# Delta rule and gated MLP on one core: state and read in one 128-column matmul, corners of two heads at a time

## The chip, the cores and the metric

The kernel runs on one core of a Trainium2 chip. The metric is the device time of one execution in microseconds; three executions of the kernel before took 574.62, 570.97 and 570.29 us, median 570.97. One more execution was taken under the hardware profiler. In its rows PE is the matrix engine (TensorE), PEld its loads of stationary operands, DVE the vector engine, ACT the scalar engine, POOL GpSimd, and SP the engine that only issues transfers.

## The reference

Two layers follow one another. The first is a delta rule per batch and head (4 batches, 8 heads, 768 tokens, head size 48), in order of the tokens, with `k` normalised:

```python
for t in range(S):
    y[:, :, t] = einsum('bhd,bhde->bhe', q[:, :, t], state)
    v_old = einsum('bhde,bhd->bhe', state, k[:, :, t])
    state = state + beta[t] * einsum('bhd,bhe->bhde', k[:, :, t], v[:, :, t] - v_old)
```

The outputs of the heads side by side are `x` (4 x 768 x 384). The second layer is a gated MLP that mixes tokens:

```python
h = gelu_tanh(x @ w_in)                 # 384 -> 1024
u, v = h[..., :512], h[..., 512:]
v_n = (v - mean(v)) / sqrt(var(v) + 1e-6) * g_ln
v_s = einsum('ts,bsd->btd', w_sg, v_n) + b_sg[None, :, None]
out = x + (u * v_s) @ w_out
```

## The kernel before

**Chunks.** The tokens are cut into chunks of 64 (`T`). There are two phases, each over two of the four batches with six chunks, so twelve chunks (`NCH`) in a row; a chunk is worked on in two halves `e = 0, 1`, and each half has two sides `sd` of eight heads. The two sides lie in partitions 0 to 63 and 64 to 127 (`TOK`; head rows in `OWN`). Every float32 matmul of the chain, the grams and the corners stands in the trace as two records, each with its weight load (384 matmuls of `own` are 768 rows).

**The triangular solve.** Inside a chunk the delta rule is a linear system with a unit triangular 64 x 64 matrix per head, made of the gram matrix of `k`. `gram` (L276) makes the grams of `k` with `k` and of `k` with `q` for the chunk seven turns ahead, in four quarters; each ends with one ACT copy of 512 elements into `GM` (L293). `gstore` sends the two 32 x 32 diagonal blocks to memory; `lanes` (L307) inverts them on DVE, one matrix per partition, as background work; `zfetch` brings the inverses into `Z`. The off-diagonal 32 x 32 block comes from two products per head, `corner_a` (L446) and `corner_b` (L461): 32 matmuls of 32 x 32 each, copied out by ACT (L459, L476). `above` (L250) masks the read matrix (the gram of `k` with `q`) on DVE.

**The chain of a chunk** (`chain`, L492), per half `e`:

- `old`: keys times the state, added on DVE to the scaled values `v` (L508);
- `ask`: queries times the state, into the bank of the read, dealt between the steps of `own`: `Z` times `v`, copied by ACT to `u` (L530);
- `state` (L536): keys times `u` (64 x 48 stationary) accumulate the state in the bank `cb`, copied by ACT to `S` (L543);
- `read` (L547): the masked matrix times `u` (64 x 64 stationary) accumulates on top of `ask`, copied by ACT to `xt` (L558). State and read are dealt step by step between one another.

**The MLP of a chunk** (`Ffn`, L648): `turn` transposes `xt` on TensorE and splits it into `xh` and `xl` (two buffers each); `values` (18 matmuls of 512 columns, named four or two at a time, L676) and `gate` (four, L640 to L642) are the projection with `w_in`, each product made of three matmuls of split operands.

**Order.** Nothing is left to a planner: every engine runs its instructions in the order in which the program names them. A loop over `TURNS` (L884) writes the order out: in each turn the steps of one chunk's chain are alternated with the MLP steps of an earlier chunk, so that TensorE has other work while ACT and DVE answer. The pair `(c, f)` names the chunk of the chain and the chunk of the MLP; turns 4 and 5 have no chain, and the transposes for the next turn's MLP are made in the turn before (L988). Background work on DVE (`lanes`, decoding of `w_in`) is let in by `tick`, by the estimates in `COST` and by `SHARE`. Loads are issued on POOL (`kload`, `qload`, `vload`, `tload`), the small transfers on SP. After the last turn follow the mixing over tokens (`spatial`) and the projection with `w_out` (`project`).

Of the kernel before, what the change touches and what calls it, by code (L numbers as in the profile page):

```python
# [21 lines left out]
T = 64  # L22
# [28 lines left out]
         *((c, c - 1) for c in range(4, NCH)), (None, NCH - 1))  # L51


@with_exitstack
def delta_rule_gmlp_kernel(
# [63 lines left out]
    GM = [(main if i < 4 else low).tile([P, NP, 2, T], F32, name=f"gm{i}") for i in range(N_M)]  # L119
# [4 lines left out]
    S = [main.tile([P, NH, HD], F32, name=f"s{i}") for i in range(N_2)]  # L124
    KT = [main.tile([P, NP, HD], F32, name=f"kt{i}") for i in range(N_2)]
# [21 lines left out]
    def tload(c):  # L147
        if c < NCH:
            load(nc.gpsimd, KT[c % N_2], ktok[c])
# [38 lines left out]
    gdt, zsrc, ztile, zds, zks, ns, nvs, ztks, j1s = {}, {}, {}, {}, {}, {}, {}, {}, {}  # L188
# [21 lines left out]

    def kgram(c):
        def phase(e):
# [9 lines left out]
            def done():  # L222
                nc.scalar.copy(out=GM[c % N_M][:, 8 * e:8 * e + 8, 0], in_=st["ps"])

# [4 lines left out]
    def gstore(c, queues):  # L229
# [5 lines left out]
        for half in range(2):  # L235
            for sd in range(2):
# [3 lines left out]
                    in_=GM[c % N_M][r0:r0 + 32, :, 0, 32 * half:32 * half + 32],  # L240
# [9 lines left out]
    def above(c):  # L250

        if c >= NCH:
            return
        m = GM[c % N_M][:, :, 1]
        nc.vector.tensor_tensor(out=m, in0=m, in1=later.unsqueeze(1).broadcast_to([P, NP, T]), op=ALU.mult)

    def qgram(c):
        def phase(e):
# [10 lines left out]
            def done():  # L269
                nc.scalar.copy(out=GM[c % N_M][:, js, 1], in_=st["ps"])  # L270

# [4 lines left out]
    def gram(c):  # L276
# [4 lines left out]
        def phase(qd):  # L281
# [10 lines left out]
            def done():  # L292
                nc.scalar.copy(out=GM[c % N_M][:, js], in_=st["ps"])  # L293
# [152 lines left out]
    def corner_a(c):  # L446
        if c >= NCH:
            return
        z, g = Z[c % N_Z], GM[c % N_M]
        j1s[c] = j1 = main.tile([P, 8, 32], F32, name="j1", bufs=2)  # L450
        ps = bank()[:, 0:256].rearrange("p (j t) -> p j t", t=32)
        for i in range(8):
            for odd in range(2):
                for sd in range(2):
                    a = slice(64 * sd + 32 * odd, 64 * sd + 32 * odd + 32)
                    b = slice(64 * sd + 32, 64 * sd + 64)
                    j = 2 * i + odd
                    mm(ps[a, i], g[b, j, 0, 0:32], z[b, j, 32:64])
        nc.scalar.copy(out=j1, in_=ps)  # L459

    def corner_b(c):  # L461
        if c >= NCH:
            return
        zx = Z[c % N_Z].rearrange("p (i x) t -> p x i t", x=2)
        j1, ztk = j1s.pop(c), ztks.pop(c)
# [677 lines left out]
```

## Time and profile before

| what | value |
|---|---|
| median of three executions | 570.97 us (570.29 to 574.62) |
| the profiled execution's own time | 572.43 us |
| its span, first to last instruction | 570.7 us |
| mean granted TensorE clock | 0.877 |
| PE busy | 452.5 us, 7763 records |
| PEld busy | 393.5 us, 7763 loads |
| DVE busy | 362.1 us, 1039 instructions |
| ACT busy | 172.5 us, 383 instructions |
| POOL busy | 83.2 us, 100 instructions |

Busy time counts an engine as busy while at least one of its instructions runs; records of TensorE overlap one another, so their lengths do not add up to its busy time. The chain of waits follows the work that ended last back to the start: at each step to what released it, or to the instruction before it on its engine. A row of the groups gives line, engine, operation, what is written from what, partitions x elements, the count, the busy time and the mean length, and the idle time before them with what ended it. For a matmul the two numbers after the tiles are rows x columns of the stationary operand.

### The profile page before, as it was taken

To read this page: it belongs to the slowest core of one execution; us is meant where nothing else is said; L and a number is where in the kernel's file an instruction comes from. 1 tells how busy PE (TensorE), PEld (TensorE's weight loads), DVE (VectorE), ACT (ScalarE), POOL (GpSimd) and SP (SyncE) were. 2 spreads that over 40 slices of the span, in tenths; PEclk is the share of its full clock that TensorE was granted. 3 is DMA by queue.
4 is the path that set the end of the run, shared out by engine and by line. 5 is a ranking of instruction groups with operands and counts; after the bars stand their busy time and mean duration, and the time that the engine had idled before them with its cause. 6 is when DMAs were issued, how large, how long until landed. Compare 5 with 4: busy or idle time off the path is not lost.

```text
span 570.7 us, 18015 instructions
## 1 busy us (share of the span) xinstructions
PE 452.5 (79%) x7763; PEld 393.5 (69%) x7763; DVE 362.1 (63%) x1039; ACT 172.5 (30%) x383; POOL 83.2 (15%) x100
## 2 busy tenths in 40 slices
PE   3134579656539762989989989799998999999997
PEld 2134356334437561878778778688997999999997
DVE  3994927316399995666987976873559657433422
ACT  2032224222234211342443444354343413111110
POOL 2311202002012000111021011000004223222220
PEclk8576669769578966788989999899999999999999
DMA  7697955449546406575684678743885762544113
GB/s 180 177 284 182 261 90 154 119 108 275 118 117 183 133 1 195 140 227 119 188 266 113 192 251 226 218 139 109 262 245 130 211 183 62 165 139 137 50 35 125
DMA packets 106239, 92.81 MB, mean 163 GB/s; under 512 B 71600, under 2 KB 83888, under 8 KB 106160
## 3 DMA queue, kind: packets, MB, share of 16 engines
q1 hardware_dynamic: 93264, 58.40, 36.8%
q0 software_dynamic: 8544, 31.72, 19.7%
q10 hardware_dynamic: 4352, 1.54, 1.1%
q8 instruction: 61, 1.00, 0.8%
q14 instruction: 18, 0.15, 0.1%
HBM read 63.30 MB, written 28.34 MB: 161 GB/s over the span
## 4 chain that ended last, share of the span: by engine, by line
PE 55%; DVE 17%; DMA 15%; issue 6%; SPq 4%; ACT 3%; ACTq 0%; POOL 0%; DVEq 0%; POOLq 0%
PE ps L81 17%; PE ps L640 10%; PE ps L642 9%; PE ps L641 9%; PE ps L676 5%; DMA z<-zd 5%; PE ps L98 3%; DVE ztmp L366 3%; DVE zl L373 3%; DMA vraw<-vD 2%; SPq L238 2%; DMA kd<-kqT 2%; DMA zd<-zl 2%; DMA zk<-zd 1%; DMA gd<-gm 1%
## 5 line engine op out<-in xcount | busy, mean ns | idle before, releaser
L81 PEld LDWEIGHTS ps<-s,kq 48*64 48x64 f32 x1408 | 49.7, 146 | 17.9 <-issue 10.8
L783 POOL TENSOR_TENSOR ga<-ga,uT 128x384 f32<-128x384 f32 x32 | 36.4, 1142 | 166.4 <-DVE ga L780 120.6
L81 PE MATMUL ps<-kd 48*64 48x128 f32 (+1 forms) x768 | 38.5, 327 | 27.5 <-DMA kd<-kqT 26.9
L81 PE MATMUL ps<-s,kq 48*64 48x48 f32 x1408 | 56.5, 232 | 0.0
L81 PEld LDWEIGHTS ps<-kd 48*64 48x64 f32 x768 | 33.2, 173 | 30.5 <-DMA kd<-kqT 20.1
L641 PE MATMUL ps<-xl,winh 128*128 128x256 f32 x144 | 43.6, 303 | 10.7 <-DVE xl L666 10.5
L366 DVE TENSOR_TENSOR ztmp<-zl 128x120 f32<-128x120 f32 (+26 forms) x180 | 48.7, 302 | 2.1
L373 DVE TENSOR_TENSOR zl<-zl,ztmp 128x120 f32<-128x120 f32 (+26 forms) x180 | 48.1, 300 | 0.8
L640 PE MATMUL ps<-xh,winh 128*128 128x256 f32 x144 | 46.8, 325 | 0.0
L508 DVE TENSOR_TENSOR v<-v,ps 128x384 f32<-128x384 f32 x22 | 12.1, 548 | 49.5 <-PE ps L81 49.5
L642 PE MATMUL ps<-xh,winl 128*128 128x256 f32 x144 | 43.1, 299 | 0.1
L645 ACT CAST gh<-ga 128x384 fp32r<-128x384 f32 x32 | 16.4, 511 | 78.9 <-POOL ga L783 63.6
L641 PEld LDWEIGHTS ps<-xl,winh 128*128 128x128 f32 x144 | 29.9, 208 | 12.3 <-DVE xl L666 12.1
L81 PE MATMUL ps<-v,z 64*64 64x48 f32 x768 | 30.4, 231 | 8.1 <-issue 4.2
L81 PE MATMUL ps<-z,gm 32*32 32x32 f32 x768 | 11.3, 208 | 32.1 <-DMA z<-zd 32.1
L646 DVE TENSOR_TENSOR gl<-ga,gh 128x384 fp32r<-128x384 f32 x32 | 18.1, 565 | 26.8 <-ACT gh L645 26.8
L81 PEld LDWEIGHTS ps<-z,gm 32*32 32x32 f32 x768 | 9.5, 119 | 35.7 <-issue 26.5
L81 PE MATMUL ps<-u,kt 64*48 64x48 f32 x704 | 23.0, 216 | 14.1 <-ACT u L530 8.9
L642 PE MATMUL ps<-wouth,gl 128*128 128x384 f32 x96 | 33.0, 347 | 1.3 <-DVE gl L646 1.3
L640 PE MATMUL ps<-wouth,gh 128*128 128x384 f32 x96 | 33.0, 346 | 1.2 <-ACT gh L645 1.2
L293 ACT COPY gm<-ps 128x512 f32<-128x512 f32 x40 | 21.8, 590 | 38.8 <-PE ps L81 31.5
L697 ACT ACTIVATE ut<-ps 128x256 f32<-128x256 f32 x48 | 18.4, 383 | 49.5 <-PE ps L642 42.1
(127 smaller groups left out, 1206.8 us busy)
## 6 DMA issues: line engine op xcount, KB each, us to landing
kq<-kqT POOLq DMA_DIRECT2D x12, 896.0 KB, 8.7
kd<-kqT POOLq DMA_DIRECT2D x10, 896.0 KB, 7.6
uD<-ut SPq DMA_DIRECT2D x12, 512.0 KB, 6.5
vD<-vg SPq DMA_DIRECT2D x24, 256.0 KB, 4.0
vraw<-vD SPq DMA_DIRECT2D x48, 128.0 KB, 3.1
uT<-uD SPq DMA_DIRECT2D x8, 768.0 KB, 5.0
v<-vtok POOLq DMA_DIRECT2D x12, 384.0 KB, 4.1
kt<-ktok POOLq DMA_DIRECT2D x12, 384.0 KB, 7.8
```

The source lines that it names most:

```text
L81: return nc.tensor.matmul(out=out, lhsT=lhsT, rhs=rhs, start=start, stop=stop, skip_group_check=True)
L98: nc.tensor.matmul(out=ps, lhsT=lhsT, rhs=busy, start=True, stop=True)
L293: nc.scalar.copy(out=GM[c % N_M][:, js], in_=st["ps"])
L366: tv.tensor_tensor(out=st["tmp"][:, at:at + m * (r1 - r0) * w].rearrange("p (m r t) -> p m r t", m=m, t=w), in0=z[:, :, r0:r1, i:i + 1].br ...
L373: tv.tensor_tensor(out=z[:, :, r0:r1, i + 1:32], in0=z[:, :, r0:r1, i + 1:32], in1=st["tmp"][:, at:at + m * (r1 - r0) * w].rearrange("p (m ...
L640: nc.tensor.matmul(out=ps, lhsT=sh, rhs=mh, start=(first and i == 0), stop=False)
L641: nc.tensor.matmul(out=ps, lhsT=sh, rhs=ml, start=False, stop=False)
L642: nc.tensor.matmul(out=ps, lhsT=sl, rhs=mh, start=False, stop=(last and i == n - 1))
L646: nc.vector.tensor_tensor(out=lo, in0=src, in1=hi.bitcast(F32), op=ALU.subtract)
L676: nc.tensor.matmul(out=self.ps, lhsT=(self.xl if k == 2 else self.xh)[:, cc, bi], rhs=(winl if k == 1 else winh)[:, cc, DH:], start=(i == ...
L697: nc.scalar.activation(out=self.ut[:, :, d].rearrange("p y e t -> p e y t"), in_=ps.rearrange("p e (y t) -> p e y t", t=T), func=AF.Gelu_a ...
L783: nc.gpsimd.tensor_tensor(out=gv, in0=gv, in1=uT[:, :, d], op=ALU.mult)
```

## The change

- `state` and `read` become one step. A tile `MK` (three of them, one per half-chunk) holds keys and masked read matrix of the eight heads in turn, 64 columns each, so that the keys of a head and its read matrix are 128 neighbouring columns, in one order for side 0 and in the other for side 1. One matmul per head and side writes state rows and read rows together. Each side has a bank of its own (`cb[sd]`), into which `ask` writes too. Both banks are copied out by ACT into `xt`, which now holds state and outputs; `S`, `KT` and the bank of the read are gone, and `xt` has two buffers for three.
- `tload` writes the keys of a half-chunk straight into `MK`, in two transfers; `above` writes the masked matrix there, half by half. The step of half 1 is moved behind `vprep`.
- The corners take two heads per matmul: `corner_a` has 64 stationary and 64 moving columns on 32 rows, of which the diagonal blocks are copied out (four copies) into a tile whose other blocks were set to zero; `corner_b` has 32 stationary and 64 moving columns on 64 rows, copied out by one copy on ACT and one on DVE.
- `GM` becomes three tiles: `GK` (columns 0 to 31 of the gram of `k`), `GE` (columns 32 to 63, two buffers) and `GQ` (the gram with `q`), by three ACT copies.
- The transposes work on 64 partitions and 64 columns each, 12 for 6. A table `TURNED` says in which turn a chunk is transposed: chunks 0 and 1 in turns 0 and 1 (before: 2 and 3), 2 and 3 in turns 3 and 4 (before: 4 and 5), the others as before.
- `xstore` is issued as two transfers; `COST` is lowered for the merged steps.

```diff
+TURNED = {0: 0, 1: 1, 3: 2, 4: 3, **{c + 2: c for c in range(4, NCH)}}
...
+    MK = [main.tile([P, 2 * NH + 1, T], F32, name=f"mk{i}") for i in range(3)]
+    J1 = [main.tile([P, 8, 2, 32], F32, name=f"j1{i}") for i in range(N_2)]
+    for t in (*MK, *J1):
+        nc.vector.memset(t, 0.0)
...
+    def tload(c, e):
+        if c >= NCH:
+            return
+        for r in range(2):
+            sd = r ^ e
+            nc.gpsimd.dma_start(
+                out=MK[(2 * c + e) % 3][TOK[r], 2 * sd:2 * sd + 2 * NH - 1:2, 0:HD],
+                in_=ktok[c, e, TOK[r]].rearrange("p (h d) -> p h d", d=HD))
...
+    def keep(c, js, ps):
+        for t, tile in enumerate((GK[c % N_M], GE[c % N_2])):
+            nc.scalar.copy(out=tile[:, js], in_=ps[:, :, 32 * t:32 * t + 32])
...
+        nc.vector.tensor_tensor(
+            out=MK[(2 * c + e) % 3][:, 1:2 * NH:2], in0=GQ[c % N_M][:, 8 * e:8 * e + 8],
+            in1=later.unsqueeze(1).broadcast_to([P, NH, T]), op=ALU.mult)
...
-                nc.scalar.copy(out=GM[c % N_M][:, js], in_=st["ps"])
+                keep(c, js, st["ps"][:, :, 0])
+                nc.scalar.copy(out=GQ[c % N_M][:, js], in_=st["ps"][:, :, 1])
...
         for i in range(8):
-            for odd in range(2):
-                for sd in range(2):
-                    a = slice(64 * sd + 32 * odd, 64 * sd + 32 * odd + 32)
-                    b = slice(64 * sd + 32, 64 * sd + 64)
-                    j = 2 * i + odd
-                    mm(ps[a, i], g[b, j, 0, 0:32], z[b, j, 32:64])
-        nc.scalar.copy(out=j1, in_=ps)
+            for sd in range(2):
+                b = slice(64 * sd + 32, 64 * sd + 64)
+                mm(ps[TOK[sd], i], g[b, 2 * i:2 * i + 2].rearrange("p x t -> p (x t)"), z[b, 2 * i:2 * i + 2, 32:64])
+        for odd in range(2):
+            for sd in range(2):
+                a = slice(64 * sd + 32 * odd, 64 * sd + 32 * odd + 32)
+                nc.scalar.copy(out=j1[a, :, odd], in_=ps[a, :, odd])
...
+            for sd in range(2):
+                mm(ps[64 * sd:64 * sd + 32, 2 * i:2 * i + 2], ztk[TOK[sd], i],
+                   j1[TOK[sd], i].rearrange("p x t -> p (x t)"))
+        for sd, copy in enumerate((nc.scalar.copy, nc.vector.tensor_copy)):
+            a = slice(64 * sd, 64 * sd + 32)
+            copy(out=z[a, :, 32:64], in_=ps[a])
...
                 for sd in range(2):
-                    r, j = sd ^ e, 8 * e + h
-                    mm(cb[OWN[sd], h], kt[TOK[r], j], u[TOK[r], j], start=(fresh[e] and h == 0))
+                    r = sd ^ e
+                    mm(cb[sd][:, h], mk[e][TOK[r], T * (2 * h + sd):T * (2 * h + sd + 2)], u[TOK[r], 8 * e + h],
+                       start=(fresh[e] and h == 0))
 
             def done():
-                mark(nc.scalar.copy(out=S[(2 * c + e + 1) % N_2][0:112], in_=cb[0:112]))
                 for sd in range(2):
+                    mark(nc.scalar.copy(
+                        out=xt[c][:, e, sd].rearrange("p (h e) -> p h e", e=HD), in_=cb[sd]))
...
-            "state0": lambda: deal(kept(0), [read(0)]),
+            "state0": lambda: deal([state(0)], []),
...
+            for y in range(2):
+                ps = bank()[:, 0:DM].rearrange("p (b c t) -> p b c t", b=2, t=T)
+                for bi in range(2):
+                    for cc in range(NC):
+                        nc.tensor.transpose(
+                            out=ps[:, bi, cc], in_=xt[self.c][TOK[y], bi, 1 - y, cc * P:(cc + 1) * P],
+                            identity=ident[TOK[y], TOK[y]])
...
-        "old0": 0.8, "old1": 0.8, "own0": 1.2, "own1": 1.2, "state0": 1.2, "state1": 1.2, "gram": 0.5,
-        "turn": 0.9, "values": 0.235, "gate": 1.05, "corner_a": 0.9, "corner_b": 0.8}
+        "old0": 0.8, "old1": 0.8, "own0": 1.2, "own1": 1.2, "state0": 0.9, "state1": 0.9, "gram": 0.5,
+        "turn": 0.9, "values": 0.235, "gate": 1.05, "corner_a": 0.7, "corner_b": 0.6}
...
             vload(c + 1)
             kload(c + AHEAD + 1)
+            tload(c + 1, 0)
         does("old0")
...
-        if n is not None:
-            above(n)
...
         feeds("gate", 1)
+        if n is not None:
+            above(n, 0)
         does("state0")
...
         if c is not None:
-            tload(c + 1)
+            tload(c + 1, 1)
...
                 turned(n)
+                above(n, 1)
...
-        if after[1] is not None:
-            turns[after[1]] = following = Ffn(after[1])
+        if at in TURNED:
+            turns[TURNED[at]] = following = Ffn(TURNED[at])
```

More of the change, by code (lines that the diff above doesn't have):

```diff
@@ L118, in delta_rule_gmlp_kernel @@
     KD = [prep.tile([112, 2, NP, T], F32, name=f"kd{i}") for i in range(N_2)]
-    GM = [(main if i < 4 else low).tile([P, NP, 2, T], F32, name=f"gm{i}") for i in range(N_M)]
+    GK = [(main if i < 4 else low).tile([P, NP, 32], F32, name=f"gk{i}") for i in range(N_M)]
+    GQ = [(main if i < 4 else low).tile([P, NP, T], F32, name=f"gq{i}") for i in range(N_M)]
+    GE = [low.tile([P, NP, 32], F32, name=f"ge{i}") for i in range(N_2)]
     Z = [main.tile([P, NP, T], F32, name=f"z{i}") for i in range(N_Z)]
@@ L222, in done @@
             def done():
-                nc.scalar.copy(out=GM[c % N_M][:, 8 * e:8 * e + 8, 0], in_=st["ps"])
+                keep(c, slice(8 * e, 8 * e + 8), st["ps"])
             return step, done
@@ L269, in done @@
             def done():
-                nc.scalar.copy(out=GM[c % N_M][:, js, 1], in_=st["ps"])
+                nc.scalar.copy(out=GQ[c % N_M][:, js], in_=st["ps"])
             return step, done
@@ L488, in delta_rule_gmlp_kernel @@
     view = lambda ps: ps[:, 0:DM].rearrange("p (h e) -> p h e", e=HD)
[L489 to L490 removed]
+    cb = [view(bank()) for _ in range(2)]
     def chain(c):
[L493 to L494 removed]
+        ks, ub, asked = {}, {}, {}
+        z, kq, u, v = (t[c % len(t)] for t in (Z, KQ, U, V))
+        mk = [MK[(2 * c + e) % 3].rearrange("p s t -> p (s t)") for e in range(2)]
         js = [slice(8 * e, 8 * e + 8) for e in range(2)]
         fresh = [c % NK == 0, False]
[L497 to L498 removed]
+        xt[c] = const.tile([P, 2, 2, DM], F32, name="x", bufs=2)
+        s_in = [(xt[c][:, 0] if e else xt[c - 1][:, 1] if c else xt[c][:, 1]).rearrange(
+            "p y (h e) -> p y h e", e=HD) for e in range(2)]
         def old(e):
@@ L706, in xstore @@
     def xstore(c):
-        nc.sync.dma_start(out=xD[c // NK][c % NK].rearrange("e p n -> p e n"), in_=xt[c])
+        for y in range(2):
+            nc.sync.dma_start(
+                out=xD[c // NK][c % NK][:, TOK[y]].rearrange("e p n -> p e n"), in_=xt[c][TOK[y], :, 1 - y])
     def norm(ph):
@@ L835, in delta_rule_gmlp_kernel @@
     vload(0)
-    tload(0)
+    for e in range(2):
+        tload(0, e)
     for c in (2, 3):
@@ L855, in delta_rule_gmlp_kernel @@
     dense(6)
-    above(0)
+    for e in range(2):
+        above(0, e)
     vprep(0)
```

70 lines of the change are left out of this document (15 added, 55 removed).

## The prediction

> **What bounds the kernel now.** I began with the page: its span and its chain of work that ended last, shared out by engine.
>
> ```profile
> span 570.7 us, 18015 instructions
> ...
> PE 55%; DVE 17%; DMA 15%; issue 6%; SPq 4%; ACT 3%; ACTq 0%; POOL 0%; DVEq 0%; POOLq 0%
> ```
>
> More than half of the chain is TensorE, but such a share is an average over stages. So I cut the run where the chain changes its engine and read the busy time of PE, PEld, DVE, ACT and POOL by stage (then granted clock, DMA share, GB/s).
>
> ```profile
> 75.00:158.00 83.00, 60.38 (x1734) 40.92 (x1728) 33.17 (x94) 24.91 (x59) 8.59 (x12) 0.77 0.59 145
> 158.00:226.00 68.00, 39.38 (x510) 33.68 (x509) 61.01 (x122) 17.77 (x41) 5.30 (x6) 0.80 0.41 122
> 226.00:400.00 174.00, 160.24 (x4001) 134.96 (x4002) 125.11 (x438) 72.93 (x183) 16.73 (x22) 0.93 0.64 183
> 400.00:571.00 171.00, 164.18 (x922) 162.07 (x920) 86.78 (x161) 38.75 (x66) 36.38 (x32) 0.99 0.48 144
> ```
>
> Up to 75 us the kernel loads and makes the first grams. From 75 to 158 run the turns of chunks 0 to 2 and the start of chunk 3. From 158 to 226 VectorE is the bound (61 of 68 us). From 226 to 400, the turns of chunks 4 to 11, TensorE is busy 160 of 174 us. The last stage holds nothing of the change. What the edit is worth is therefore read from the third stage, and there from the chain in order of time (start, length, what). One turn, chunk 8, in part:
>
> ```profile
> 323.74 1.08 PE ps L81 x55
> 324.82 1.12 PE ps L676 x4
> 325.94 1.06 PE ps L81 x32
> ...
> 332.83 0.68 PE ps L81 x50
> ...
> 334.64 0.66 PE ps L662 x6
> ...
> 335.75 0.68 PE ps L81 x50
> ```
>
> At 323.74 stand state and read of one half (64 records; the chain names only some), at 324.82 four value products, at 325.94 `old` (32 records), at 332.83 and 335.75 the two corner products (64 records each), at 334.64 the transposes. Piece follows piece: what TensorE gains or loses here moves the end by as much.
>
> The three rows with 64, 32 and 64 records already speak: 64 records take 1.08 us, 32 take 1.06, another 64 take 0.68. The number of records does not set the time. What does is seen inside the state phase, in the list of instructions (start, length, engine, line; `kt` is the state update, `gm` the read):
>
> ```profile
> 323.67 0.25 PE L81 MATMUL ps<-u,kt 64*48 64x48 f32 x2
> 323.68 0.26 PE L81 MATMUL ps<-u,gm 64*64 64x48 f32 x2
> ...
> 324.39 0.21 PE L81 MATMUL ps<-u,kt 64*48 64x48 f32 x2
> 324.42 0.40 PE L81 MATMUL ps<-u,gm 64*64 64x48 f32 x8
> ```
>
> State update and read lie on different quarters of the array, two quarters each, and run beside one another, 16 records to a quarter. They start together; the updates end at 324.60, the reads at 324.82. Less the first record, 15 steps take 0.68 us and 0.88 us: 45 ns and 59 ns a record. Both stream 48 columns of `u`; they differ only in the stationary tile, 48 columns against 64. So each stationary column costs (59-45)/16 = 0.85 ns, and the weight load sets the pace. The loads' own lengths agree (the groups of weight loads between 321 and 341 us):
>
> ```profile
> L642 PEld LDWEIGHTS ps<-xh,winl 128*128 128x128 f32 x12 | 2.3, 189 | 0.0
> ...
> L81 PEld LDWEIGHTS ps<-u,gm 64*64 64x64 f32 x64 | 2.0, 135 | 0.1
> L81 PEld LDWEIGHTS ps<-u,kt 64*48 64x48 f32 x64 | 1.7, 120 | 0.1
> ```
>
> From 64 to 128 columns a load grows by 54 ns, 0.84 per column. A long stream costs the same per column; this gram phase is 32 records on four quarters, 8 each, with 64 stationary and 128 moving columns:
>
> ```profile
> 92.04 1.10 PE L81 MATMUL ps<-kd 48*64 48x128 f32 x32
> ```
>
> With some 0.3 us for the first record, 7 steps take 0.8 us, 0.11 us each. One rule covers all: a quarter's step is about 0.84 ns times the larger of stationary and moving columns, plus 5 ns; a phase is 15 steps plus 0.2 us. It gives 1.08 for state and read, and for the corners (32 by 32: 32 ns) 0.68. Both are the chain's rows.
>
> **The change, part by part.** State and read: per half-chunk 32 matmuls (64 records) on four quarters become 16 (32 records) on two row halves, with 128 stationary columns and the same 48 moving. A step costs 0.84 x 128 + 5 = 112 ns, there are still 16 per tile, and the phase takes 15 x 0.112 + 0.2 = 1.9 us, for 1.08: +0.85 us. The four quarters already did both jobs at once; the merged form gives that up, for it loads the 128 columns one after another. Bounds: if only the stream counted, 15 x 0.045 + 0.2 = 0.9 us (-0.2); if the load could not lie under its own tile's stream, a step is 107 + 40 + 5 = 152 ns and the phase 2.5 us (+1.4). I take +0.85, since the two row kinds above already pace by their loads and already hide the stream.
> [...]
>
> Corners: each product goes from 64 records on four 32x32 tiles to 32 records on two tiles, 16 each, with 64 moving columns (half of what is computed is thrown away). A step costs 0.84 x 64 + 5 = 59 ns for 32, the product 1.08 us for 0.68: +0.4 each, +0.8 per chunk. This needs no new kind of row: `old`, 16 steps on each of two tiles with 64 columns, takes 1.06.
>
> Transposes: 12 of 64 moving columns for 6 of 128. By the same rule 12 x 59 = 0.7 us for 0.66: nothing. The first two move into the turns of chunks 0 and 1.
>
> Third stage: 16 state phases x 0.85 = 13.6, eight pairs of corners (chunks 4 to 11) x 0.8 = 6.4: +20.0 us.
>
> Second stage, 75 to 158, whose chain has these rows among others (the first belongs to the stage before):
>
> ```profile
> 31.61 2.06 ACT gm L293 x4
> ...
> 100.25 4.93 issue
> ...
> 135.54 13.32 DMA z<-zd
> ```
>
> Here the state phases of chunk 0, and the first of chunks 1 and 2, stand before something that waits (3.4 us); the others lie under waits for `z` such as that of 13.32 us. The four corner pairs add 3.2, and the transposes come in twice and go out once (+0.7). Sum +7.3, of which the waits may swallow half: 3.6 to 7.3; I take 6, since each wait for `z` begins only after TensorE's own part. From 158 to 226 TensorE has room: 0.
>
> ACT and DMA:
>
> ```profile
> L293 ACT COPY gm<-ps 128x512 f32<-128x512 f32 x40 | 21.8, 590 | 38.8 <-PE ps L81 31.5
> L697 ACT ACTIVATE ut<-ps 128x256 f32<-128x256 f32 x48 | 18.4, 383 | 49.5 <-PE ps L642 42.1
> ...
> kt<-ktok POOLq DMA_DIRECT2D x12, 384.0 KB, 7.8
> ```
>
> From these two rows a copy costs 0.18 us plus 0.81 ns an element. The gram's one copy of 512 becomes 128 + 128 + 256: 0.28 + 0.28 + 0.38 = 0.94 us for 0.59, 40 times: 14 us of ACT, busy 73 of 174 us in the third stage, so hidden behind the value products that follow. If that cover went, the four gram quarters of the third stage would cost 1.4, the 16 in the turns of chunks 0 to 3 5.6. Before 75 us the four copies at 31.61 would take 3.8 us for 2.06; the loads behind them are late anyhow: +1, between 0 and 3. A corner's `j1` takes four copies (1.5 us for 0.4), with value products and transposes (1.12 + 0.66) as cover; the `z` copies go from four to one each on ACT and DVE. DVE's clearing of the new tiles at the start falls into the first load. `ktok` comes in four transfers per chunk, in pieces of one head's row; each has most of a turn (20 us) against 7.8 us to landing.
>
> New waits: POOL's second pair of `tload` waits for the first state phase of its turn, with the next `vload` and `kload` queued behind it, which nobody needs for a turn. The masked read matrix for the second half is written on DVE after `vprep`, ahead of the copy of `z`; should it also wait for that transfer, up to 2 us a turn would come on top. The gram's second tile has two buffers, so ACT waits for the store of two chunks before; that counts only before 75 us and lies in the bound of 3. At chunk 3 the third pair of `xh`, `xl` is asked for while two are in use: ACT's casts wait for a gram and six value products (1.1 + 1.7 us), with DVE's subtraction behind them: 0 to 2.8 us, taken as 0, since DVE lags there.
>
> Given back: what TensorE waited for, first in 75 to 226, then in the third stage (total, times, longest):
>
> ```profile
> PE ps L81 <- issue: 5.8, 3, 4.9
> ```
>
> ```profile
> PE ps L81 <- issue: 6.8, 4, 2.6
> PE ps L81 <- DVE v L508: 1.9, 1, 1.9
> PE ps L81 <- ACT ut L697: 1.8, 3, 1.1
> ```
>
> "Issue" is time without a visible wait, 12.6 us in all. The change drops 704 + 768 records and adds 72, a fifth of those from 75 to 400. If the stalls go with the instructions to bring in, a third may go: -4, between 0 and -12.6. Of the 3.7 us behind DVE and ACT a slower TensorE sees less: -1.5, between 0 and -3.7.
>
> Sum: 20.0 + 6 + 1 - 4 - 1.5 = +21.5 us. The profiled execution took 572.4 us (span 570.7, 1.7 around it), 1.4 above the median of the three runs: 572.4 + 21.5 = 594, and as a median 592.5 us. With each unknown at its end the forecast's own range is 578 (20 + 3.6 - 12.6 - 3.7 = +7.3, less the 1.4) to 604 (21.5 and 1.3, 2, 4, 1.5, 2.8: +33).
>
> **The rivals.** First, the other side: records are what costs. State phase and corners then lose half their steps at the old pace: 0.2 + 7 x 0.059 = 0.6 (-0.47) and 0.2 + 7 x 0.032 = 0.4 (-0.26). Over 20 exposed state phases and 24 corner products that is -9.4 - 6.2, with half of the issue stalls -6: 549 us. It decides if a step with 128 stationary columns stays under about 60 ns. Against it stand 32 records in 1.06 us beside 64 in 1.08; for it only the issue stalls. Chance 0.06. [...]
>
> Second, the 128-column load is not the limit and only the stream counts: state -0.2 x 20 = -4, corners +0.8 x 12 = 9.6, stalls -6: about 571. The loads' lengths speak against it. Chance 0.10.
>
> Third, loads no longer hide (step of 152 ns), or DVE's new wait costs 2 us a turn: 11 (0.55 x 20) to 16 us (2 x 8) more, 603 to 608. Chance 0.10.
>
> Fourth, the change does not do what it says where it counts: TensorE's extra time in the third stage is taken up by its 14 us of idle there, and the early part by waits: 20 - 14 + 1 - 4 = +3: 574 us. The idle is spread over many short gaps, which speaks against. Chance 0.06.
>
> **How the numbers follow.** The forecast keeps 0.68, at 592 us. Faster by over 1% (about the least that these runs can tell, below 565) comes from the first rival and a third of the second: 0.10. Within 1%: the rest of the second and most of the fourth, 0.11. Slower by over 1% (above 577): 0.79. The range 573 to 606 leaves out the first rival, most of the second and a part of the third: about 0.2.
>
> **What would show it.** Right: state phases of 32 records lasting 1.9 us with weight loads near 190 ns, corner products of 1.1 us, about 6360 records for 7763, turns from 301 to 341 us grown from 20 to about 22.5 us, the last stage unchanged. Wrong: a state phase of 1.1 us or less (second or first rival), one of 2.5 (third), a DVE wait for a `ktok` transfer in every turn, or turns that grow by less than the phases do (fourth). The "issue" sum tells the size of what is given back.

## The result and the profile after

The changed kernel takes 595.01 us (median of four executions, 592.31 to 603.38), the kernel before 570.63 us beside it: ratio 1.0403, 95% interval 1.0324 to 1.0483. Put on a chip a second time it took 597.43 us against 572.12 (ratio 1.0476, 1.0394 to 1.0559). The change costs some 24 to 25 us. (Ratios here and below leave out slow executions, such as that of 603.38 us; a median is over all.) The profiled execution took 592.31 us, 590.6 of them its span.

The page of the changed kernel: span and instructions, busy time of the engines, and the chain of work that ended last by engine.

```profile
span 590.6 us, 15401 instructions
...
PE 486.2 (82%) x6344; PEld 426.1 (72%) x6363; DVE 375.7 (64%) x1067; ACT 180.1 (30%) x469; POOL 108.1 (18%) x136
...
PE 61%; DVE 14%; DMA 10%; issue 8%; ACT 3%; SPq 2%; ACTq 0%; POOL 0%; DVEq 0%; POOLq 0%
```

TensorE has 1419 records fewer than before and is busy 34 us longer. Why, one turn shows (L82 is the helper that issues every small matmul, L81 before), read in the chain in order of time (start, length, what; the turn with chunk 10's chain):

```profile
385.62 1.92 PE ps L82 x32
387.54 1.12 PE ps L677 x4
388.66 1.06 PE ps L82 x32
...
390.87 1.08 PE ps L82 x64
...
396.40 1.08 PE ps L82 x32
...
398.61 0.69 PE ps L659 x12
...
399.96 1.01 PE ps L82 x32
```

At 385.62 stands the merged state and read: 32 records, 1.92 us, where 64 took 1.08. At 396.40 and 399.96 stand the two corner products, 1.08 and 1.01 us for 0.68. `old` (388.66), `own` with `ask` (390.87), the value products (387.54) and the transposes (398.61) are as long as before. The weight loads of the merged step, in the groups of weight loads between 385 and 409 us (busy, mean ns):

```profile
L82 PEld LDWEIGHTS ps<-u,mk 64*128 64x128 f32 x96 | 5.6, 188 | 0.4
```

Each phase is as long as the prediction made it. Whether the stages follow is another question. The answer of the profile by stage (busy time of PE, PEld, DVE, ACT, POOL; granted clock; DMA share; GB/s), first the kernel before, then the changed one. The cuts are the first state phase of chunk 0, the first corner product of chunk 4, and the end of the last state phase:

```profile
83.40:226.50 143.10, 91.84 (x2062) 68.96 (x2063) 94.62 (x216) 39.80 (x92) 13.89 (x18) 0.80 0.50 137
226.50:396.50 170.00, 156.74 (x3979) 131.81 (x3979) 122.81 (x432) 69.89 (x175) 16.73 (x22) 0.93 0.65 185
396.50:570.70 174.20, 167.68 (x945) 165.22 (x943) 88.64 (x164) 41.79 (x73) 36.38 (x32) 0.99 0.48 144
```

```profile
80.40:225.90 145.50, 102.51 (x1622) 80.40 (x1639) 99.77 (x232) 41.88 (x122) 23.03 (x31) 0.80 0.53 140
225.90:416.80 190.90, 179.72 (x3061) 152.36 (x3061) 129.49 (x448) 71.99 (x184) 29.88 (x41) 0.92 0.60 163
416.80:590.60 173.80, 167.88 (x949) 164.88 (x949) 88.41 (x164) 41.99 (x74) 36.22 (x32) 0.99 0.48 143
```

The third stage grew by 20.9 us, the second by 2.4, the last by nothing, and the prologue came out 3 us shorter. So far this looks like a forecast that came true, 20.0 for 20.9 in the stage that matters. The experiments say that it is one only in part.

They need one more way of reading such a row. The length of a stage is TensorE's work at full clock, plus what the throttle adds, plus idle time. In the traces of the two kernels every stretch of the clock record is whole or half (the rows under experiment 5 show 1.00 and 0.50). With the clock taken so in every run, a mean of 0.92 over 190.9 us means that 0.08 x 190.9 = 15.3 us of the busy time were added by half-clock stretches. So the third stage after is 179.7 - 15.3 = 164.4 us of work, 15.3 of throttle and 11.2 idle; before it was 144.8, 11.9 and 13.3. The clock is given to two digits, so each split is good to about 0.9 us. The mean also counts half clock that falls into TensorE's idle time, where it adds nothing. In the third stage that puts up to 2.4 us too much into the throttle and too little into the work (most in experiment 3, whose two half-clock stretches last 19.5 us and hold 15.3 us of TensorE's work). In the second stage, with long waits at half clock, it is far more, so there only busy and idle time are compared. I call throttle and idle together the lost time: 25.2 us before, 26.5 after.

### The profile page after: what moved, and what is told of

It is laid out like the page before. It is cut to its first block, busy times and chain, and to the rows that moved or that the text cites. A ratio compares the mean times of both kernels' runs of the same rounds, so it can differ in the third digit from the quotient of the medians.

```text
span 590.6 us, 15401 instructions
## 1 busy us (share of the span) xinstructions
PE 486.2 (82%) x6344; PEld 426.1 (72%) x6363; DVE 375.7 (64%) x1067; ACT 180.1 (30%) x469; POOL 108.1 (18%) x136
## 3 DMA queue, kind: packets, MB, share of 16 engines
q0 software_dynamic: 9504, 31.72, 19.6%
## 4 chain that ended last, share of the span: by engine, by line
PE 61%; DVE 14%; DMA 10%; issue 8%; ACT 3%; SPq 2%; ACTq 0%; POOL 0%; DVEq 0%; POOLq 0%
PE ps L82 23%; PE ps L637 10%; PE ps L639 9%; PE ps L638 9%; PE ps L677 6%; DMA kd<-kqT 5%; PE ps L99 3%; DVE zl L389 2%; DVE ztmp L382 2%; DMA vraw<-vD 2%; PE ps L659 1%; DMA z<-zd 1%; DVE vraw L758 1%; DVE zl L410 1%; DMA zd<-zl 1%
## 5 line engine op out<-in xcount | busy, mean ns | idle before, releaser
L82 PEld LDWEIGHTS ps<-x,kq 48*64 48x64 f32 x1408 | 51.5, 149 | 17.1 <-issue 11.4
L82 PE MATMUL ps<-kd 48*64 48x128 f32 (+1 forms) x768 | 40.0, 346 | 28.0 <-DMA kd<-kqT 28.0
L82 PE MATMUL ps<-u,mk 64*128 64x48 f32 x768 | 51.5, 286 | 12.1 <-ACT u L540 9.1
L82 PEld LDWEIGHTS ps<-u,mk 64*128 64x128 f32 x768 | 48.3, 200 | 17.3 <-ACT u L540 11.9
L82 PE MATMUL ps<-x,kq 48*64 48x48 f32 x1408 | 58.5, 235 | 0.5 <-issue 0.5
L82 PEld LDWEIGHTS ps<-kd 48*64 48x64 f32 x768 | 34.8, 190 | 30.6 <-DMA kd<-kqT 19.3
L157 POOL DMA_DIRECT2D mk<-ktok x48 | 33.1, 695 | 111.1 <-PE ps L82 110.7
L638 PE MATMUL ps<-xl,winh 128*128 128x256 f32 x144 | 42.3, 294 | 0.7 <-DVE xl L667 0.7
L82 PE MATMUL ps<-v,z 64*64 64x48 f32 x768 | 31.1, 234 | 10.7 <-issue 8.9
L82 PE MATMUL ps<-z,gk 32*64 32x64 f32 x384 | 16.7, 243 | 27.5 <-DMA z<-zd 27.5
L82 PEld LDWEIGHTS ps<-z,gk 32*64 32x64 f32 x384 | 14.9, 154 | 30.9 <-issue 29.4
L82 PEld LDWEIGHTS ps<-v,z 64*64 64x64 f32 x768 | 27.9, 149 | 12.2 <-issue 9.9
L555 ACT COPY x<-ps 128x384 f32<-128x384 f32 x48 | 20.7, 483 | 46.1 <-PE ps L82 46.1
```

What stands on the lines that cost most here:

```text
L82: return nc.tensor.matmul(out=out, lhsT=lhsT, rhs=rhs, start=start, stop=stop, skip_group_check=True)
L157: nc.gpsimd.dma_start(out=MK[(2 * c + e) % 3][TOK[r], 2 * sd:2 * sd + 2 * NH - 1:2, 0:HD], in_=ktok[c, e, TOK[r]].rearrange("p (h d) -> p ...
L555: mark(nc.scalar.copy(out=xt[c][:, e, sd].rearrange("p (h e) -> p h e", e=HD), in_=cb[sd]))
L638: nc.tensor.matmul(out=ps, lhsT=sh, rhs=ml, start=False, stop=False)
```

## The experiments

**1. State and read split again.** In the changed kernel each 128-column matmul becomes two of 64 columns into the same places:

```diff
-                    mm(cb[sd][:, h], mk[e][TOK[r], T * (2 * h + sd):T * (2 * h + sd + 2)], u[TOK[r], 8 * e + h], ...)
+                    for w in range(2):
+                        b = 2 * h + sd + w
+                        mm(cb[sd][TOK[w], h], mk[e][TOK[r], T * b:T * b + T], u[TOK[r], 8 * e + h], ...)
```

> The changed kernel, but each 128-column state-and-read matmul is issued as two of 64 stationary columns, one for each half of the columns, into the same places of the same two banks; everything else stays, the output too. Theory (loading 128 stationary columns in a row paces the phase): two column halves load beside one another again, a state phase of 64 records takes 1.08 us in place of 32 records in 1.92. In the third stage (226 to 420 us, chunks 4 to 11) 16 phases x 0.85 = 13.6 us less, before it 0 to 3.4 us less: 595.0 - 13.6 = 581 us, 578 to 582. Rival (the number of records costs): 512 records more make it no faster, 595 us or more, and stalls without a visible wait grow. Rival (the cost lies elsewhere in the change, in waits or copies): within 3 us of 595.

574.65 us, ratio 1.0035 (0.9990 to 1.0081). In the chain a state phase of 64 records is back at 1.08 us:

```profile
385.96 1.08 PE ps L82 x64
```

By the ratios, 768 records more (512 of them in the third stage) make the kernel some 20 us faster, so the number of records is not what costs. But 20 is more than the 13.6 us that the phases are worth, so something else is paid along with them.

**2. The corners of before** in the changed kernel: one head per matmul, one ACT copy after the first product, four after the second.

```diff
-                mm(ps[TOK[sd], i], g[b, 2 * i:2 * i + 2]..., z[b, 2 * i:2 * i + 2, 32:64])
+                mm(ps[a, i], g[b, j], z[b, j, 32:64])
...
-                mm(ps[64 * sd:64 * sd + 32, 2 * i:2 * i + 2], ztk[TOK[sd], i], j1[TOK[sd], i]...)
+                mm(ps[odd][a, i], ztk[r, i], j1[r, i])
```

> The changed kernel with the corner products of the kernel before: one head to a matmul, 32 by 32 on four tiles, one ACT copy after the first and four after the second; the merged state update and the rest stay. Theory (the longer of stationary and moving columns paces a tile, so the two-head form doubles the steps' price and halves their number on half the tiles): a product takes 0.68 us in place of 1.08 (first) and 1.01 (second), eight pairs in the third stage x 0.75 = 6.0 us less, the four pairs before it hidden or 3 us less: 595.0 - 6 = 589 us, 586 to 590. Rival (records cost): no gain or slower, 595 to 600. Rival (the four small ACT copies of the new first product are what costs, 1.5 us for 0.4): then the gap between the end of the first product and the start of the second shrinks by about 1 us as well, 8 us more, 581.

574.89 us, ratio 1.0063 (1.0027 to 1.0099): again some 20 us less, under all three figures expected, where the products are worth 6. The third theory, the four small ACT copies, is not the reason: they stay in place in experiments 6 and 7, which find the surplus elsewhere.

**3. Both edits.**

> Both edits together: split state matmuls and one-head corners in the changed kernel. What is left of the change then is the gram kept in three tiles, the state held with the outputs, the transposes in halves and in other turns, and the read matrix in the other layout. Theory: the two gains add, 13.6 + 6 = 19.6 us less: 575 us, 571 to 577, so the left-over parts cost 0 to 6 us against the kernel before (570.6). If the left-over parts cost more (three gram copies, pieces of the key transfer, the wait of VectorE): 580 or more. If records were what costs: 600 or more.

569.96 us, ratio 0.9983 (0.9941 to 1.0024), just under what was expected. The parts of the change that are left (three gram tiles, keys in four transfers, the layout of the read matrix, transposes in halves and in other turns) cost nothing. But 20 and 20 don't add: together the two edits give some 25. Something is paid in the changed kernel only when both forms meet.

**4. A longer stream.** The moving side of each state matmul gets 48 zero columns, added to the next head's, so the output stays.

```diff
-   ... u[TOK[r], 8 * e + h], ...
+   ... u[TOK[r], j:NP + 1:NP - j], ...      # the columns of head j, then zeros
```

> The changed kernel, but each state matmul streams 96 columns in place of 48: the second 48 are zeros, added to the next head's columns, so the output stays. Loads of 128 stationary columns are as before. Theory (a tile's step is the longer of the two, here still 128 stationary columns): phases stay at 1.92 us, the time at 595 us, within 2. Rival (load and stream of a tile follow one another): a step grows by 48 x 0.84 = 40 ns, a phase by 0.6 us, 16 phases in the third stage 9.7 us and up to 2.4 before it: 605 to 607. Rival (only the stream counts): the step goes from what 48 columns take to what 96 take, the same 40 ns, 605 to 607 as well.

590.72 us, ratio 1.0352 (1.0296 to 1.0408), not longer than the changed kernel, but 2 us below the range expected; why it is shorter was not shown. The phase, in the chain:

```profile
392.76 1.96 PE ps L82 x32
```

Twice the stream costs 0.04 us a phase (1.96 for 1.92), which is one longer last stream (48 columns at the prediction's 0.84 ns). So the 128 stationary columns pace the phase here, and 96 moving ones lie under them. With experiment 1 this settles the mechanism of the prediction for the phase.

**5. The changed kernel a second time**, for the places of its lost time.

> The changed kernel again, unaltered, beside the kernel before on the chip of this call, as the base for the comparisons, and for a second look at where its half-clock stretches lie. Theory (the stretches come from TensorE's waits for VectorE, which sit at fixed places of the program): waits of 1 to 3.5 us ahead of the own products of chunks 7, 8, 9 and 11 again, and 7 to 17 us of half clock behind them; 590 to 596 us, ratio 1.035 to 1.043. The prologue can lie up to 6 us later than in the first profile, where the first corner product did not wait for the second transfer of z. Rival (the stretch of 306 to 320 us was chance): no half clock between 245 and 375 us, and a profiled run about 6 us shorter in the third stage.

597.43 us, a little above the figures expected. Its third stage is the first profile's over again:

```profile
233.90:424.80 190.90, 179.71 (x3061) 152.26 (x3061) 129.71 (x448) 72.17 (x184) 29.88 (x41) 0.92 0.61 164
```

190.90 us both times, with the same clock and the same busy time, and the slice of its page from 313.5 to 328.5 us has a clock of 0.5, where the half-clock stretch of 306.6 us falls if it stands 8.0 us later, as the whole stage does. So its lost time is no chance; it sits at fixed places. One of them, in the first profile. First the chain, then VectorE's instructions in order (start, length, line, operation):

```profile
378.07 0.39 ACT ut L698
378.46 3.33 issue
381.79 1.95 PE ps L82 x60
```

```profile
376.74 0.69 DVE L487 COPY z<-ps 32x512 f32<-32x512 f32 x1
377.45 0.36 DVE L596 TENSOR_TENSOR f<-f,wouth 128x192 f32<-128x192 f32 x1
...
380.20 0.69 DVE L689 BATCH_NORM_STATS2 bs<-vg 128x6 f32<-128x512 f32 x1
380.92 0.18 DVE L690 BATCH_NORM_AGGREGATE mv<-bs 128x2 f32<-128x6 f32 x1
381.13 0.56 DVE L520 TENSOR_TENSOR v<-v,ps 128x384 f32<-128x384 f32 x1
```

The chain calls the gap of 3.33 us "issue", as if nothing were waited for. But `own` needs the `v` of L520, which VectorE comes to only at 381.13, after other work of its queue without a gap, and 0.1 us after it ends TensorE goes on. The gaps at 303.5 and 333.1 us end in the same way. Earlier in the queue, at all three, stands L487, the copy of the second corner product into `z` that the change gave to VectorE. And what can follow such a wait, seen at the one of 303.5 us by windows:

```profile
302.00:306.60 4.60, 2.65 (x75) 2.36 (x74) 4.43 (x18) 0.51 (x2) 0.00 (x0) 1.00 1.07 277
306.60:320.20 13.60, 13.60 (x147) 11.41 (x147) 6.83 (x31) 1.89 (x5) 1.47 (x3) 0.50 0.09 20
320.20:330.00 9.80, 9.80 (x137) 8.09 (x135) 4.39 (x12) 5.78 (x17) 2.76 (x4) 1.00 0.63 181
```

VectorE is busy 4.43 of 4.60 us, TensorE only 2.65; then come 13.6 us at half clock, though TensorE is busy all through them. Not every wait is followed so. Behind the one of 3.33 us at 378.5 stand 3.4 us of half clock, and behind the one at 333.1 none, for the next state phase takes its full-clock time:

```profile
333.06 1.45 issue
...
336.91 1.92 PE ps L82 x32
```

Of the stretches behind these waits one lasts 3.4 us and the other 13.6, four times that. The longer one stands behind the shorter wait (1.7 us for 3.3), and TensorE was busy for all of its 13.6 us before the clock rose. What decides when the clock falls and when it rises was not shown.

**6. The copy taken from VectorE.** In the changed kernel ScalarE makes both copies of the second corner product.

```diff
-        for sd, copy in enumerate((nc.scalar.copy, nc.vector.tensor_copy)):
+        for sd, copy in enumerate((nc.scalar.copy, nc.scalar.copy)):
```

> The changed kernel, but ScalarE makes both copies of the second corner product into z; VectorE, which made one of the two (0.69 us a chunk), makes none. The first runs gave 590.7 us for a kernel that keeps the changed matmuls, and 574.9 us with the corners as before, 16 us less where the products alone are worth 6 to 7. Theory: the rest is the VectorE copy. In the third stage TensorE waits for VectorE's queue (the v additions), and each such wait is followed by a stretch of half clock (306 to 320 us in the changed kernel, none there with the old corners). Then this edit gives 5 to 9 us: 582 to 587 us, and the half clock at 306 to 320 us is gone. Rival (the half-clock stretch came by chance, or from the products themselves): within 2 us of 591 to 595. Rival (ScalarE's second copy comes later still, as it lies on the way to the next turn): 1 to 4 us more.

582.53 us, ratio 1.0194 (1.0134 to 1.0253): 12 to 15 us less than the changed kernel in its two times on a chip, and more than the 5 to 9 us expected, which were reckoned from experiment 4's 590.7 us. The third stage:

```profile
227.30:406.30 179.00, 172.11 (x3061) 145.93 (x3061) 123.52 (x440) 76.70 (x192) 29.79 (x41) 0.96 0.64 174
```

Work is the same (172.1 - 0.04 x 179.0 = 164.9 us, for 164.4). The lost time is not: 14.1 us for 26.5. Half clock makes up 14.3 us of the stage for 30.5 (twice 0.04 x 179.0 and twice 0.08 x 190.9), about as much less as the stretches behind the waits at 303 and 378 us hold (13.6 and 3.4). VectorE's copies, in the groups of the changed kernel in the third stage:

```profile
L487 DVE COPY z<-ps 32x512 f32<-32x512 f32 x8 | 5.5, 690 | 6.5 <-ACT z L487 6.3
```

The copies take 5.5 us in all. The 6.5 us of idle time ahead of them are no price: 6.3 of them are one wait, ahead of the copy at 232.2 us, and without that copy VectorE stands there for 7.3 us all the same, until TensorE has made what the next `v` needs. What costs is that each copy delays the `v` behind it, for which `own` waits: TensorE's idle time at the three places of experiment 5 is 0.98, 0.69 and 2.01 us here, for 1.96, 1.68 and 3.56 there. Of the 12.4 us of lost time, 4.3 are idle time (11.2 to 6.9) and 8.1 are half clock (15.3 to 7.2).

**7. The same with split state**, the missing corner of a cube.

```diff
+ split state matmuls (1) and both copies on ScalarE (6); two-head corner products stay
```

> The changed kernel with split state matmuls and with both copies of the second corner product on ScalarE; the corner products stay in the two-head form. It is the missing corner of a cube: merged or split state, VectorE copy or none, with two-head corners throughout (merged with the copy 595 to 597 us, merged without it 582.5, split with it 574.7). Theory (the copy costs 12 us in the merged form alone, where TensorE's longer phases make VectorE's queue wait at it and TensorE then waits for what is queued behind; with split state there is slack for it): 571 to 576, ratio 1.000 to 1.010. Rival (the copy takes 12 us of VectorE's time whatever the state does): 561 to 565, ratio 0.982 to 0.990, which would beat both kernels.

569.11 us, ratio 0.9966 (0.9934 to 0.9997). That lies between the two figures expected. The copy costs 4 to 5.5 us beside split state (the first by the ratios, the second by 574.65 for 569.11) and 12 to 15 beside the merged one. The two-head corner products then cost nothing (569.11 for the 569.96 of experiment 3), though TensorE's work shows them. This is the fastest form that was run, 0.3% under the kernel before, with an interval that just leaves out no change.

The third stage in experiments 2, 1, 7 and 3, one row of each kernel:

```profile
223.60:400.10 176.50, 166.61 (x3573) 140.56 (x3573) 122.55 (x440) 70.77 (x184) 29.85 (x41) 0.96 0.64 175
```

```profile
227.80:407.00 179.20, 165.06 (x3573) 137.95 (x3573) 129.72 (x448) 72.12 (x184) 29.81 (x41) 0.92 0.65 174
```

```profile
222.80:394.60 171.80, 162.76 (x3573) 135.93 (x3573) 123.30 (x440) 76.97 (x192) 29.80 (x41) 0.94 0.67 182
```

```profile
226.30:395.30 169.00, 155.70 (x4085) 129.06 (x4085) 122.81 (x440) 70.82 (x184) 29.80 (x41) 0.94 0.68 183
```

Split as above, with the work over the 144.8 us of before and what the prediction's phases give for that kernel:

| kernel | state | corner products | copy on VectorE | work, over before | phases say | lost time | time, ratio |
|---|---|---|---|---|---|---|---|
| before | split | one head | no | 0 | 0 | 25.2 | 1 |
| 3 | split | one head | no | +0.7 | 0 | 23.4 | 0.998 |
| 7 | split | two heads | no | +7.6 | 6.4 | 19.4 | 0.997 |
| 1 | split | two heads | yes | +5.9 | 6.4 | 28.5 | 1.004 |
| 2 | merged | one head | no | +14.7 | 13.6 | 17.0 | 1.006 |
| 6 | merged | two heads | no | +20.1 | 20.0 | 14.1 | 1.019 |
| changed | merged | two heads | yes | +19.6 | 20.0 | 26.5 | 1.040, 1.048 |

Two things are seen. The work follows the phases everywhere, within 1.3 us as it is split here. And the lost time shrinks as work is added (23.4, 19.4, 17.0, 14.1 in the rows without the copy), and jumps by 9 to 12 us where VectorE makes the copy. In those four rows TensorE's idle time is 13.3, 9.0, 9.9 and 6.9 us and its clock 0.94, 0.94, 0.96 and 0.96. I read this so: longer phases take up time in which TensorE otherwise waits for VectorE, and in the two rows with merged state less goes to half clock too (7.1 and 7.2 us, for 10.1 and 10.3 in experiments 3 and 7); why the clock was higher there was not shown. About 8 us of added work are then free, and the rest comes through one for one. By the ratios (1% is 5.7 us) against experiment 3: 6.4 us of phases cost -1 us, 13.6 cost 5, 20.0 cost 12. Nothing here shows which share of the free time is clock and which is waits; the two trade places. Nor is one profile exact. Experiment 1's row comes from an execution of 580.11 us, 5.5 above its median, so its 28.5 is too high for the time beside it. And experiment 8's kernel, whose third stage has the same instructions as experiment 3's, shows 178.1 us there for 169.0, in an execution of 582.37 us, 8 above its median. The order of the rows rests on the times beside them.

```profile
228.80:406.90 178.10, 162.08 (x4085) 134.32 (x4085) 123.01 (x440) 70.72 (x184) 29.86 (x41) 0.90 0.65 175
```

**8. The early part alone.** Changed forms for chunks 0 to 3, split state and one-head corners from chunk 4 on.

```diff
+                    if c < 4:
+                        mm(cb[sd][:, h], ... 128 columns ...)
+                        continue
+                    for w in range(2): ... 64 columns ...
+        if c < 4:
+            return corner_a_two(c)      # and corner_b_two
```

> Split state matmuls and one-head corners from chunk 4 on, the changed forms (128-column state matmuls, two-head corners with their copies) for chunks 0 to 3 alone. So only the stages before 226 us differ from the run with both edits, which took 570.0 us, ratio 0.998 to the kernel before. The prediction's step: 3.4 us of state phases and 3.2 us of corners there, most of which reaches the end: 4 to 6 us more, 574 to 576, ratio 1.006 or more. Rival, which the profile after suggests (the third stage began at 225.9 us, in the kernel before at 226.5): waits for z and VectorE's substitution swallow it all: within 1.5 us of 570, ratio 0.998.

Ratio 0.9958 (0.9901 to 1.0014). The median is 574.4 us, and its executions spread from 563 to 582, more than those of any other kernel here. The median speaks for the prediction's step, the ratio for the rival, so by the time alone this decides nothing. The second stage in its profile, and in that of experiment 3:

```profile
85.10:228.80 143.70, 101.38 (x1623) 79.30 (x1640) 98.42 (x228) 41.85 (x122) 22.98 (x31) 0.79 0.52 139
```

```profile
86.10:226.30 140.20, 94.18 (x2087) 69.60 (x2087) 95.00 (x219) 41.13 (x122) 22.97 (x31) 0.79 0.53 143
```

The stage is 3.5 us longer: TensorE is busy 7.2 us more (101.4 for 94.2) and idle 3.7 us less (42.3 for 46.0). In this pair about half of what was added was taken from its waits.

**9. More early work.** Experiment 3's kernel with `N_FILL = 6` for 3.

> The kernel with both edits (split state matmuls, one-head corners), but with six in place of three filler matmuls (128 by 512, BF16) at each of the twelve places in a turn where no gated-MLP work is there to be dealt: turns of chunks 0 to 2, 8 calls each with at least 0.215 us a matmul, so 24 x 3 x 0.215 = 15.5 us more TensorE work at full clock before 150 us. If TensorE's own time in that stage reaches the end at 0.8 of its length, as the prediction took it: 12 us more, 582. If VectorE and the fetches of z set the pace there: 0 to 4 us more, 570 to 574, with waits for z shorter by what was added. A gain of up to 3 us is possible where the filler keeps the clock up.

576.23 us, ratio 1.0104 (1.0048 to 1.0160), so 6 to 7 us above experiment 3. The second stage, though, hardly moved:

```profile
85.50:227.00 141.50, 98.95 (x2131) 70.57 (x2153) 95.40 (x219) 41.22 (x122) 22.98 (x31) 0.87 0.53 142
```

The fillers are 15.5 us of work by the estimate above (in the kernel before, three take 0.82 us, the last record 0.38 of it: 0.22 each), but TensorE is busy only 4.8 us longer (98.95 for 94.18), for its clock rose from 0.79 to 0.87. Its idle time fell by 3.5 us (42.5 for 46.0) and the stage grew by 1.3. So most of the added work was paid for by the clock that it kept up, and 3.5 us of it by the waits; the run does not show what waits alone would take up. What the time rose by all the same stands, as far as the profile shows it, in the third stage (from 227.0 to 399.7 us, 172.7 for 169.0), which was not edited; why, stays open.

**10. The clock kept up.** Experiment 3's kernel with 20 fillers that VectorE lets go when it has ended the substitution of chunks 4 to 7.

```diff
+            if at == 5:
+                nc.vector.memset(kick, 0.0)
+                keep_warm(bank(), 20, kick)
```

> The kernel with both edits, and 20 filler matmuls more (128 by 512, BF16) ahead of the corners of chunk 4, held back until VectorE has ended the substitution of chunks 4 to 7 (at about 218 us), so that they run while TensorE waits for z (until 226 us). Nothing else differs. Theory (a stretch of half clock follows each long wait of TensorE, and costs half of its length in the third stage): the clock is granted in full at 226 us in place of 235.6 us, which gives up to 4.8 us: 565 to 568 us, ratio to the kernel before 0.988 to 0.994. Rival (the filler ends after z has come): 0 to 4 us more, 570 to 574. Rival (the granted clock does not pace this code): 570, unchanged.

576.10 us, ratio 1.0084 (1.0046 to 1.0122): slower by under 1%. The third stage of its profile:

```profile
218.70:390.00 171.30, 154.77 (x4086) 128.20 (x4085) 124.33 (x442) 71.46 (x188) 29.80 (x41) 0.96 0.67 180
```

The clock did come up (0.96 for 0.94) and less was lost to it (6.9 us for 10.1), but idle time grew from 13.3 to 16.5 us, and the stage by 2.3. A faster TensorE waited more instead. That fits the table: the lost time is as much idle time as clock. The profiled execution is the fastest of the twelve, 566.06 us, which lies in the theory's range; but the clock did not bring that, for its first state phase began 7.9 us earlier than in experiment 3 (78.2 for 86.1), ahead of all that this edit touches.

**11. VectorE relieved by GpSimd.** Experiment 3's kernel with the masking of the read matrix on GpSimd.

```diff
-        nc.vector.tensor_tensor(
+        nc.gpsimd.tensor_tensor(
             out=MK[(2 * c + e) % 3][:, 1:2 * NH:2], in0=GQ[c % N_M][:, 8 * e:8 * e + 8], ...
```

> The kernel with both edits (split state matmuls, one-head corners; 570.0 us, ratio 0.998), with the masking of the read matrix moved from VectorE (0.67 us, two a chunk) to GpSimd, where a product of two tiles of 384 columns takes 1.14 us, so about 1.5 us each. Theory (TensorE's waits in the third stage are for VectorE's queue, 4 to 8 us there, with half clock behind some of them): 16 x 0.67 = 10.7 us of VectorE's 123 us in that stage go, and the time falls by 2 to 6 us: 564 to 568, ratio 0.988 to 0.994. Rival (VectorE's queue is not what the waits are for): within 2 us of 570. Rival (GpSimd's issue of key and value transfers stands behind the products, and both engines slow one another on the same tiles): 2 us or more slower.

585.54 us, ratio 1.0253 (1.0197 to 1.0309): 15 us slower. Groups of VectorE over the whole run, of experiment 3 and then of this one (L267 is the masking):

```profile
L381 DVE TENSOR_TENSOR ztmp<-zl 128x120 f32<-128x120 f32 (+26 forms) x180 | 49.0, 303 | 2.0
...
L267 DVE TENSOR_TENSOR mk<-gq,later 128x512 f32<-128x512 f32 x24 | 16.0, 670 | 0.0
...
L370 DVE SCALAR_TENSOR_TENSOR zl<-zl 128x25 f32<-128x25 f32 (+5 forms) x86 | 14.7, 246 | 0.3
```

```profile
L381 DVE TENSOR_TENSOR ztmp<-zl 128x120 f32<-128x120 f32 (+26 forms) x180 | 53.0, 326 | 2.0
...
L370 DVE SCALAR_TENSOR_TENSOR zl<-zl 128x25 f32<-128x25 f32 (+5 forms) x86 | 18.1, 285 | 0.3
```

The same instructions became 8 and 16% longer (326 ns for 303, 285 for 246), and VectorE, rid of 16.0 us of work, was busy 371.9 us in all for 364.5. Both groups read two inputs, as the products on GpSimd do (24 of 1.29 us). But not all such groups grew so: L388, which also reads two, went from 302 to 311 ns, and L789, from the last stage, where no masking is left, from 610 to 611. What made the two groups longer was not shown. How much of the 15 us is this and how much the transfers queued on GpSimd behind the products was not separated.

## Why the prediction was right, and where it was not

The time came within 3 us of the forecast, in the forecast's direction, and the mechanism that it named is there. That the sum came so near is in part luck, for two errors of some 10 us cancel in it. Point by point:

- **State phase, +0.85 us: right.** 1.92 us measured for 1.9, with loads of 188 ns for about 190; experiments 1 and 4 leave nothing to the rivals of "records" and "stream". The third rival's dearer step (2.5 us) is excluded by the phase itself.
- **Corner product, +0.4 us: right** as a phase (1.08 and 1.01 for 1.08). **Transposes, 0.7 us: right** (0.69). Records: 6344 for "about 6360". Last stage unchanged: 173.8 for 174.2.
- **Third stage, +20.0 us: the size right, the reason half right.** It grew by 20.9, but two unpriced things of 8 to 12 us cancel in it. The failing step is "the `z` copies go from four to one each on ACT and DVE", which was costed at nothing, with no work named that hides it: the copy on VectorE cost 12 us in the stage's lost time and 12 to 15 us in time. The other failing step is in the fourth rival, put aside because "the idle is spread over many short gaps": 8 to 11 us of the added work did go into lost time where VectorE was left alone, so without the copy the same 20 us of phases would have cost 9 in this stage (179.0 for 170.0).
- **"Issue" given back, -4 us: wrong in kind.** It was 6.8 us before and 7.4 after. The label was read as a stall of instruction supply that goes with the records. At 303, 333 and 378 us of the changed kernel it is `own` waiting for `v`, with VectorE's queue late; the view knows no releaser, and the reader has to look at the other engines' instructions. The longest of the kernel before, 2.6 us, is of the same kind: it ends at 365.48, 0.1 us after the `v` of L508. The waits put down to `v` and `ut` did shrink, from 3.7 to 1.5 us for the -1.5 forecast, but with "issue" a wait for `v` too the two terms can't be told apart. TensorE's idle time in the stage fell by 2.1 us in all (13.3 to 11.2).
- **Second stage, +6 us (3.6 to 7.3): too much.** +2.4 us, in the profiles of both executions. TensorE is busy 10.7 us longer there (102.5 for 91.8) and idle 8.3 us less (43.0 for 51.3). The failing step is "I take 6, since each wait for `z` begins only after TensorE's own part": most of what was added went into waiting time. The pair of experiment 8 shows less of this, half.
- **Prologue, +1 us (0 to 3): not to be read from one profile.** Chunk 0's first state phase began 3.0 us earlier than before in the first profile and 5.0 later in the second (88.4 us), with the transfer that brings `z` of chunk 0. The chain shows the wait for it before and in the second profile, and none in the first, where the same transfers had landed by 73.07:

```profile
66.87 7.90 DMA z<-zd
```

```profile
71.59 6.70 DMA z<-zd
```

  This and 1.4 us in the last stage are what the two profiled executions (592.31 and 598.99 us) differ by. In nine of the ten other kernels made from the changed one this phase began between 83.8 and 86.6 us, some 2 us later than before.

With the second profile in mind the sum reads: prologue about +2, second stage +2.4, third +20.9, last -0.4, which is 25 us for the 24.4 and 25.3 between the medians. The forecast's 21.5 had 20 + 6 + 1 - 4 - 1.5.

## What to carry to other kernels

Here the merging of two column tiles of small FP32 matmuls into one stationary operand of 128 columns halved the records (32 for 64) and gave up loading the tiles beside one another: 1.92 us a phase for 1.08. The step is longer by its loads (112 ns for 59, by the prediction's estimate from the rows) and not by its stream, so that was the price, and it could be computed from the loads' rows. Price every instruction that a change adds to an in-order queue on which the critical engine waits, even one of 0.7 us (here 12 us of lost time), by what stands behind it, and look there for every gap that a view can't name. And a term that comes out right in its sum is not yet shown right: undo its parts one at a time and see whether they add.

## What the runs showed of the hardware

- The half clock behind a wait can cost more than the wait: 1.7 us of waiting at 303.5 us were followed by 13.6 us at half clock (the second profiled execution has a slice at 0.5 there too), while 1.45 us at 333.1 were followed by none. In the long stretch a state phase took 3.58 us for 1.92:

```profile
308.40 3.58 PE ps L82 x32
311.98 2.00 PE ps L677 x4
```

- The same program can have one stage alike to the last digit in two executions (190.90 us), while its prologue differs by 8 us (80.4 and 88.4).
- With products of two inputs moved to GpSimd, two groups of VectorE's two-input instructions became 8 and 16% longer, a third 3% (experiment 11). VectorE was then busy longer in all than with the work that it had given away.
